# Decode attention with a streamed output projection: wo of two neighbouring groups in one transfer and one projection

## The chip, the cores and the metric

The kernel runs on one core of one Trainium2 chip. The metric is the device time of one execution in microseconds (us); lower is better. Each run also has a "span": the time from the first to the last instruction that the profile of that run shows, usually 1.2 us below the device time and free of what happens outside the program.

## The reference, cut to what matters

Two independent problems, A and B, are computed and concatenated. Each is one decode step of attention over the last 4096 keys of a cache, followed by an output projection.

```python
B, Sq, D = 2, 1, 576
Hq, Hkv, Sk, Dh = 32, 16, 16384, 128
W = 4096
q = (x @ wq)                                   # 2 rows, 32 heads of 128
k = repeat(k_cache[:, :, Sk - W:, :], 2)       # 16 kv heads, 4096 keys
v = repeat(v_cache[:, :, Sk - W:, :], 2)
p = softmax(q k^T * Dh ** -0.5)
o = p v
return o.reshape(B, Sq, Hq * Dh) @ wo          # wo: 4096 x 576
```

K and V are read once, 134 MB in all, and wq and wo are 19 MB more. There is little arithmetic for each byte.

## The kernel before

The work is cut into 8 groups (4 per problem) of 4 kv heads, that is 8 query heads, and a group into 2 slabs, one per batch row. A slab of K or V is one 4 MiB transfer (128 rows of 32 KB) into a ring of four slots. For each group there is also one "stripe" of wo, 1024 rows of 576 numbers: 128 partitions with 8 wo rows each, so 9 KB per partition. All these transfers go out on one queue in a fixed order:

```python
for t in range(NSLAB + LAG):                    # NSLAB = 16, LAG = 3
    if t < NSLAB:
        stream.append(("K", t))
    if t >= LAG:
        i = t - LAG
        if i % 2 == 0 and 0 < i // 2 < NG - 1:
            stream.append(("W", i // 2 - 1))    # a stripe of wo
        stream.append(("V", i))
stream.append(("W", NG - 2))                    # stripe 6
stream.append(("W", NG - 1))                    # stripe 7
# ... (cut)
if kind == "W":
    sl = i % 2                                  # two buffers of 8 rows
    rows = probs[P][4][gl * 1024:(gl + 1) * 1024, :].rearrange("(p j) n -> p j n", j=8)
    deps = [proj_op[i - 2]] if i >= 2 else []
    cuts = [(0, 8, wo_sem[sl])]
    if i == NG - 2:                             # stripe 6 in two pieces
        cuts = [(0, 4, wo_sem[sl]), (4, 8, lastw_sem[2])]
    elif i == NG - 1:                           # stripe 7 in three: 4, 3 and 1 rows
        cuts = [(w_cuts[k], w_cuts[k + 1], ([wo_sem[sl]] + lastw_sem)[k]) for k in range(3)]
```

`make_PV` multiplies the softmax weights with a slab of V. After the last V slab of a group, VectorE (DVE) reduces the result, PE multiplies it with a selection matrix (`make_dg`, "the select" below), and DVE masks and picks O into the layout that the projection needs (`make_pick`). The projection is 8 rows times 2 halves of the output, 16 matmuls of 288 columns.

The end of the program, in the order in which PE gets it:

```python
make_PV(i + 3, (0,))          # last V slab, first piece
make_dg(NG - 1, (0,)); make_pick(NG - 1, (0,))
filler(2)                     # two matmuls whose result nobody reads
make_PV(i + 3, (1, 2))        # last V slab, the other two pieces
make_evac(i + 3)
filler(2)
make_dg(NG - 1, (1,))         # the last select, waits for VectorE
make_pick(NG - 1, (1,))
make_proj(NG - 2)             # stripe 6
make_proj(NG - 1)             # stripe 7
make_E(NPROB - 1)             # copy out, output transfer
```

Of the kernel before, what the change touches and what calls it, by code (L numbers as in the profile page):

```python
# [62 lines left out]
def build_kernel(nc, probs, out):  # L63
# [29 lines left out]
    with es:  # L93
        sb = lambda name, shape, dt: es.enter_context(nc.sbuf_tensor(name, shape, dt))
        ring = sb("ring", [128, NSLOT, SW], BF16)
        xt = sb("xt", [128, 2, HW_], BF16)
        wob = sb("wob", [128, 2, 8, NOUT], BF16)
        zq = sb("zq", [128, 4, 4, 144], BF16)
        pR = sb("pR", [128, 2048], BF16)
        pT = sb("pT", [128, 2, 2048], BF16)  # L100
# [15 lines left out]
        jmask_f = sb("jmask_f", [128, 8], FP32)  # L116
        m8 = sb("m8", [128, 16, 8], FP32)
        selx = sb("selx", [128, 8, 16], FP32)
        bsel = sb("bsel", [128, 2], FP32)
        hmask = sb("hmask", [8, 2], FP32)  # L120
        mx = sb("mx", [128, 2], FP32)
# [7 lines left out]
        ssum = sb("ssum", [128, 2], FP32)  # L129
        rsb = sb("rsb", [128, 2, 2], FP32)  # L130
        oP = sb("oP", [128, 2, 8, Bb], BF16)
        part = sb("part", [Bb, NH], FP32)
        out_sb = sb("out_sb", [Bb, NPROB, NOUT], BF16)
        STT = [es.enter_context(nc.psum_tensor("st%d" % i, [128, 1024], FP32)) for i in range(2)]
# [20 lines left out]
        v_cuts = [0, 64, 112, KJ]  # L155
        lastv_sem = [sem("lastv%d" % k) for k in range(2)]
        w_cuts = [0, 4, 7, 8]
        lastw_sem = [sem("lastw%d" % k) for k in range(3)]
        wq_sem = [sem("wq%d" % P) for P in range(NPROB)]
        wo_sem = [sem("wo%d" % r) for r in range(2)]  # L160
        x_sem = sem("xload")
# [63 lines left out]
        p_v2 = pool(lambda e: e.tensor_tensor(v2[:], vmask[:, 0:2], vmask[:, 2:4], ALU.add), [d_vm], "v2")  # L225
        p_m8 = pool(lambda e: e.tensor_copy(m8[:], jmask_f[:, 0:8].unsqueeze(1).broadcast_to([128, 16, 8])), [d_jf], "m8")
        p_sx = pool(lambda e: e.tensor_copy(selx[:], jmask_f[:, 0:8].unsqueeze(2).broadcast_to([128, 8, 16])), [d_jf], "selx")

        tbn = [0]
        tb_consumer = {}  # L230
# [86 lines left out]
        for t in range(NSLAB + LAG):  # L317
            if t < NSLAB:
                stream.append(("K", t))
            if t >= LAG:  # L320
                i = t - LAG
                if i % 2 == 0 and 0 < i // 2 < NG - 1:
                    stream.append(("W", i // 2 - 1))
                stream.append(("V", i))
        stream.append(("W", NG - 2))
        stream.append(("W", NG - 1))
        slot_of = {}
        uses = {}
        n_slot = 0
        for key in stream:  # L330
            if key[0] != "W":
                slot_of[key] = (n_slot + 3) % NSLOT
                uses.setdefault(slot_of[key], []).append(key)
                n_slot += 1
# [1 line left out]
        stream_dma = {}  # L336
        last_reader = {}
        pos = [0]
        proj_op = {}

        def issue(key):
            kind, i = key
            if kind == "W":
                P, gl = i // GP, i % GP
                sl = i % 2
                rows = probs[P][4][gl * 1024:(gl + 1) * 1024, :].rearrange("(p j) n -> p j n", j=8)
                deps = [proj_op[i - 2]] if i >= 2 else []
                cuts = [(0, 8, wo_sem[sl])]
                if i == NG - 2:
                    cuts = [(0, 4, wo_sem[sl]), (4, 8, lastw_sem[2])]  # L350
                elif i == NG - 1:
                    cuts = [(w_cuts[k], w_cuts[k + 1], ([wo_sem[sl]] + lastw_sem)[k]) for k in range(3)]
                stream_dma[key] = []
                for j0, j1, sm in cuts:
                    def f(e, j0=j0, j1=j1, sm=sm):
                        return e.dma_start(wob[:, sl, j0:j1, :].rearrange("p j n -> p (j n)"),
                                           rows[:, j0:j1, :].rearrange("p j n -> p (j n)")).then_inc(sm, 16)
                    stream_dma[key].append((j0, j1, dma_op("sp", sm, 1, f, deps, "wo%d_%d" % (i, j0))))
                return
            P, g, b = i // (2 * GP), (i // 2) % GP, i % 2  # L360
            src_t = probs[P][1] if kind == "K" else probs[P][2]
            src = src_t[b, 4 * g:4 * g + 4, Sk - W:Sk, :].rearrange("k (r j) d -> r k j d", j=KJ)
            r = slot_of[key]
            prior = uses[r][:uses[r].index(key)]
            deps = [last_reader[prior[-1]]] if prior else first_deps[r]
            cuts = [(0, KJ, ring_sem[r])]
            if key == ("V", NSLAB - 1):
                cuts = [(v_cuts[k], v_cuts[k + 1], ([ring_sem[r]] + lastv_sem)[k]) for k in range(3)]
            stream_dma[key] = []
            for c0, c1, sm in cuts:  # L370
                def f(e, c0=c0, c1=c1, sm=sm):
                    return e.dma_start(ring[:, r, c0 * 128:c1 * 128],
                                       src[:, :, c0:c1, :].rearrange("r k j d -> r k (j d)")).then_inc(sm, 16)
                stream_dma[key].append((c0, c1, dma_op("sp", sm, 1, f, deps, "%s%d_%d" % (kind, i, c0))))
# [187 lines left out]

        def make_dg(G, bs=(0, 1)):
            b0, nb = bs[0], len(bs)
            n, bank, op = tb_job(lambda e, bank: e.matmul(bank[:, 0:128 * nb], selx[:].rearrange("p h c -> p (h c)"),  # L565
                                                          oR[:, b0:b0 + nb, :].rearrange("p b d -> p (b d)"), start=True, stop=True),
                                 "dg%d_%d" % (G, b0), [ch[(G, "red%d" % b)] for b in bs] + [p_sx])
            ch[(G, "dg")] = op
            dg_job[(G, bs)] = (n, bank)

        def make_pick(G, bs=(0, 1)):
            v = G % 2
            b0, nb = bs[0], len(bs)
            n, bank = dg_job[(G, bs)]
            tv = tmp[:, 0:128 * nb]
            a = dve(lambda e: e.tensor_tensor(
                tv.rearrange("p (b c j) -> p b c j", b=nb, c=16), bank[:, 0:128 * nb].rearrange("p (b c j) -> p b c j", b=nb, c=16),
                cm16[:, 0:16].unsqueeze(1).unsqueeze(3).broadcast_to([128, nb, 16, 8]), ALU.mult), [ch[(G, "dg")], d_cm, ch["tmp"]], "A%d" % G)
            tb_consumer[n] = a

            def f_pick(e):
                with nc.allow_low_precision(reason="one term of the sixteen is not zero"):
                    return e.tensor_reduce(oP[:, v, :, b0:b0 + nb].rearrange("p j b -> p b j"),
                                           tv.rearrange("p (b c j) -> p b j c", b=nb, c=16), AX.X, ALU.add)
            ch[(G, "oP", b0)] = dve(f_pick, [a] + ([proj_op[G - 2]] if G >= 2 else []), "oP%d_%d" % (G, b0))
            ch["tmp"] = ch[(G, "oP", b0)]

        def make_proj(G, part=None):
            P = G // GP
            v = G % 2  # L590
            start = G % GP == 0
            ensure(("W", G))
            oPs = [ch[(G, "oP", b)] for b in range(2) if (G, "oP", b) in ch]
            parts = stream_dma[("W", G)]
            for j0, j1, dma in parts if part is None else [parts[part]]:
                split = G == NG - 1 and j1 == 8
                for halves in ([(0,), (1,)] if split else [(0, 1)]):
                    def f(e, j0=j0, j1=j1, halves=halves):
                        for j in range(j0, j1):
                            wt = oP[:, v, j, :]  # L600
                            for h in halves:
                                mv_ = wob[:, v, j, h * NH:(h + 1) * NH]
                                if h == 1 and G >= NG - 2:
                                    last = e.matmul(PJL, wt, mv_, start=G == NG - 2 and j == 0, stop=True, skip_group_check=True)
                                elif h == 1:
                                    last = mm_held(e, PJ[h], wt, mv_, start and j == 0, ((128, 32), (0, 0)))
                                else:
                                    last = e.matmul(PJ[h], wt, mv_, start=start and j == 0, stop=True, skip_group_check=True)  # L608
                        return last
                    deps = oPs + [dma]  # L610
                    if start:
                        deps += [e_ops[(P - 1, 0)], e_ops[(P - 1, 1)]] if P >= 1 else [q_ev[2]]
                    op = pe(f, deps, "proj%d_%d" % (G, j0))
                    if split:
                        projh[halves[0]] = op
                    else:
                        proj_op[G] = op

        def make_part():
            ch["part"] = act(lambda e: e.activation(part[:], PJ[1], ACTF.Copy), [proj_op[NG - 3]], "part")  # L620

        def make_E(P):
            if P < NPROB - 1:
                d = [proj_op[(P + 1) * GP - 1]]
                e_ops[(P, 0)] = dve(lambda e: e.tensor_copy(out_sb[:, P, 0:NH], PJ[0]), d, "Elo%d" % P)
                e_ops[(P, 1)] = act(lambda e: e.activation(out_sb[:, P, NH:NOUT], PJ[1], ACTF.Copy), d, "Ehi%d" % P)
            else:
# [10 lines left out]
        for t in range(NSLAB):  # L638
# [26 lines left out]
                make_sums(Gs)  # L665
            if Gd is not None:
                make_dg(Gd)
            if Gp is not None:
                make_proj(Gp)
                if (Gp + 1) % GP == 0:  # L670
                    make_E(Gp // GP)
            if Gc is not None:
# [10 lines left out]
        make_bias(NG - 1)  # L683
        make_PV(i + 1)
        make_evac(i + 1)
        make_proj(NG - 3)
        make_part()
        make_dg(NG - 2)
        make_pick(NG - 2)
# [105 lines left out]
```

## Time and profile before

| | before |
|---|---|
| device time, median of 3 runs | 363.62 us (363.46 to 364.47) |
| span of the profiled run | 362.1 us |
| bytes read from HBM | 153.10 MB, 423 GB/s over the span |
| busy: PE, DVE, ACT | 65%, 59%, 13% |

The page of the profile, the rows of PE clock and DMA (one digit per fortieth of the span, in tenths) and the DMA packets:

```profile
PEclk9999699969898768969899889969698966898959
DMA  8999999999999999999999999999999999999996
DMA packets 6803, 153.26 MB, mean 423 GB/s; under 512 B 764, under 2 KB 904, under 8 KB 1544
```

The DMA row is at 9 from the second slice to the last but one. The core is a DMA stream with some arithmetic beside it. The PE clock moves between 6 and 9 tenths. These are means over a slice: the clock records of all traces hold only two values, 1.0 (full) and 0.5 (half), and all but the last of a trace, which the end cuts, are multiples of 3.41 us long.

The transfers of wo, with KB and the median time from issue to landing:

```profile
wob<-in_A_wo_dram SPq DMA_DIRECT2D x4, 1152.0 KB, 30.4
wob<-in_B_wo_dram SPq DMA_DIRECT2D x2, 1152.0 KB, 31.1
```

A transfer lands 30 us after its issue although it moves in 2.76 to 2.78 us (from the first engine's landing of the transfer ahead to its own): the queue was full.

The chain of work that ended last, its last pieces (start, duration, what):

```profile
340.44 19.13 DMA wob<-in_B_wo_dram
359.61 0.28 PE pj L608
...
360.26 0.05 PE pj L604
360.33 0.45 DVE out_sb L629
```

The chain names the last piece of wo but one, which landed at 359.57; the last one, a single row, landed at 359.92, in time for its matmuls at 359.97. So the run ends with the wo landings, a few matmuls, the copy. The timeline of PE there (start, duration, instruction, idle time before it in brackets):

```profile
356.35 0.49 PE L565 MATMUL tb<-oR,selx 128*128 128x128 f32 x2 [1.11 <-DVE oR L555]
356.77 0.28 PE L608 MATMUL pj<-wob,oP 128*2 128x288 bf16 x1
...
357.63 0.29 PE L604 MATMUL pj<-wob,oP 128*2 128x288 bf16 x1
358.67 0.28 PE L608 MATMUL pj<-wob,oP 128*2 128x288 bf16 x1 [0.76 <-DMA wob<-in_B_wo_dram]
...
359.61 0.28 PE L608 MATMUL pj<-wob,oP 128*2 128x288 bf16 x1 [0.28 <-DMA wob<-in_B_wo_dram]
...
359.98 0.29 PE L604 MATMUL pj<-wob,oP 128*2 128x288 bf16 x1
```

The last select ran at 356.35, then stripe 6 (16 matmuls, two at a time every 0.12 us). Then PE idled before stripe 7, whose two bracketed waits name the wo transfer. The tail followed the data.

Two waits that the prediction uses, one of the DMA queue's own and one of DVE:

```profile
SPq L356 <- PE pj L244: 10.7, 1, 10.7
```
```profile
313.55 0.23 DVE L484 SCALAR_TENSOR_TENSOR bias<-vmask,tb,offm 128x4 f32<-128x4 f32 x1 [7.60 <-PE tb L481]
```

For finer questions I use two kinds of record in the trace that have no view of their own: each DMA packet with its size, start and duration, and each of the 16 semaphore increments of a transfer (one per DMA engine), called landings below.

### The profile page before, as it was taken

The numbers are of one execution on the slowest core, as the hardware profiler recorded it, in microseconds if no ns is written. First come the engines' busy times: TensorE is split into PE (matmuls) and PEld (weight loads), VectorE is DVE, ScalarE is ACT, GpSimd is POOL, SyncE is SP. The second block draws the span as 40 slices with busy tenths as digits, with TensorE's granted clock in tenths as the row PEclk, the third lists the DMA queues.
The fourth block names the chain that finished last, engine by engine and source line by source line (L and its number), as shares of the span: only waits on it lengthen the run. The fifth ranks groups of instructions, "written<-read, shape, count | busy, mean of one in ns | idle before, by whom it ended". The sixth has DMA issues, their size and how long they took to land.

```text
span 362.1 us, 2631 instructions
## 1 busy us (share of the span) xinstructions
PE 234.5 (65%) x1294; PEld 57.2 (16%) x935; DVE 211.9 (59%) x141; ACT 46.1 (13%) x80; POOL 22.0 (6%) x82
## 2 busy tenths in 40 slices
PE   0397788567654957665684836665786627849575
PEld 0010111112110211211120201212121201202222
DVE  0201898495949093764939185772939367393732
ACT  1002100140041000500032000500005000320500
POOL 3100101100010000100010000100010001000000
PEclk9999699969898768969899889969698966898959
DMA  8999999999999999999999999999999999999996
GB/s 327 456 427 413 456 411 438 431 420 449 416 436 434 420 449 400 450 434 424 443 418 427 442 420 447 420 427 442 420 430 434 431 438 424 429 434 427 418 414 256
DMA packets 6803, 153.26 MB, mean 423 GB/s; under 512 B 764, under 2 KB 904, under 8 KB 1544
## 3 DMA queue, kind: packets, MB, share of 16 engines
q1 hardware_dynamic: 6772, 153.10, 98.7%
q8 instruction: 8, 0.13, 0.1%
q14 instruction: 3, 0.02, 0.0%
q10 hardware_dynamic: 20, 0.01, 0.0%
HBM read 153.10 MB, written 0.00 MB: 423 GB/s over the span
## 4 chain that ended last, share of the span: by engine, by line
DMA 54%; DVE 23%; PE 13%; issue 8%; ACT 1%; POOL 0%; ACTq 0%; SPq 0%
DMA ring<-in_B_k_cache_dram 32%; DMA ring<-in_A_k_cache_dram 14%; DVE xt L427 13%; DMA wob<-in_B_wo_dram 5%; PE st L244 4%; DMA tmp<-in_B_x_dram 3%; PE pj L244 3%; PE st L453 3%; DVE mx L461 2%; DVE oR L559 2%; ACT pR L491 1%; DVE tmp L552 1%; PE ot L275 1%; DVE pT L500 1%; PE ot L530 1%
## 5 line engine op out<-in xcount | busy, mean ns | idle before, releaser
L453 PE MATMUL st<-xt,zq 128*128 128x512 bf16 x256 | 120.9, 472 | 95.7 <-DVE xt L427 95.7
L427 DVE STREAM_TRANSPOSE xt<-ring 128x4096 f32<-128x4096 f32 x32 | 141.6, 4430 | 40.1 <-DMA ring<-in_A_k_cache_dram 23.4
L244 PE MATMUL st<-xt,zq 128*128 128x512 bf16 x256 | 119.6, 467 | 0.0
L491 ACT ACTIVATE pR<-st,bias 128x512 bf16<-128x512 f32 x32 | 40.0, 1419 | 227.5 <-DVE bias L484 227.5
L453 PEld LDWEIGHTS st<-xt,zq 128*128 128x128 bf16 x256 | 28.6, 112 | 216.6 <-DVE xt L427 112.6
L530 PE MATMUL ot<-ring,pT 128*32 128x512 bf16 x512 | 33.9, 408 | 2.9 <-DVE ssum L514 1.8
L484 DVE SCALAR_TENSOR_TENSOR bias<-vmask,tb,offm 128x4 f32<-128x4 f32 x8 | 1.8, 224 | 38.0 <-PE tb L481 38.0
L514 DVE TENSOR_REDUCE ssum<-tb 128x2 f32<-128x8 f32 x8 | 1.3, 162 | 36.8 <-PE tb L511 36.8
L500 DVE STREAM_TRANSPOSE pT<-pR 128x2048 bf16<-128x2048 bf16 x8 | 18.4, 2303 | 1.1 <-ACT pR L491 1.1
L419 POOL TENSOR_TENSOR zq<-qs,bmask 128x64 bf16<-128x64 bf16 x32 | 8.7, 294 | 163.2 <-PE st L244 140.9
L559 DVE TENSOR_REDUCE oR<-tmp 128x128 f32<-128x512 f32 x15 | 15.7, 1045 | 0.5
L530 PEld LDWEIGHTS ot<-ring,pT 128*32 128x32 bf16 x512 | 12.8, 100 | 19.3 <-DMA ring<-in_B_v_cache_dram 5.7
L552 DVE SCALAR_TENSOR_TENSOR tmp<-ot,rsb,dmask 128x512 f32<-128x512 f32 x16 | 11.5, 718 | 6.5 <-PE ot L530 6.5
L608 PE MATMUL pj<-wob,oP 128*2 128x288 bf16 x64 | 14.4, 285 | 1.0 <-DMA wob<-in_B_wo_dram 1.0
L244 PE MATMUL pj<-wob,oP 128*2 128x288 bf16 x48 | 12.0, 286 | 0.0
L244 PE MATMUL pj<-ring,pT 128*32 128x512 bf16 x36 | 11.8, 412 | 0.0
L254 PE MATMUL tb<-ident_b,pR 8*128 8x8 bf16 x9 | 0.7, 198 | 14.2 <-DVE pR L215 14.2
L461 DVE TENSOR_REDUCE mx<-st 128x2 f32<-128x1024 f32 x8 | 9.7, 1215 | 0.0
L491 ACT ACTIVATION_READ_ACCUMULATOR pR<-st,bias 128x1 f32 x32 | 9.0, 282 | 0.0
L565 PE MATMUL tb<-oR,selx 128*128 128x256 f32 (+1 forms) x18 | 6.2, 427 | 2.7 <-DVE ssum L514 1.5
L215 DVE TENSOR_TENSOR pR<-tmp,hmask 8x1152 bf16<-8x1152 bf16 x1 | 1.3, 1346 | 11.2 <-DMA tmp<-in_B_x_dram 11.2
L275 PE MATMUL ot<-ring,pT 128*32 128x512 bf16 x18 | 7.5, 419 | 0.5 <-ACT pT L261 0.5
(64 smaller groups left out, 71.0 us busy)
## 6 DMA issues: line engine op xcount, KB each, us to landing
ring<-in_A_k_cache_dram SPq DMA_DIRECT2D x8, 4096.0 KB, 28.0
ring<-in_A_v_cache_dram SPq DMA_DIRECT2D x8, 4096.0 KB, 30.1
ring<-in_B_k_cache_dram SPq DMA_DIRECT2D x8, 4096.0 KB, 28.9
ring<-in_B_v_cache_dram SPq DMA_DIRECT2D x7, 4096.0 KB, 30.6
ring<-in_A_wq_dram SPq DMA_DIRECT2D x1, 4608.0 KB, 13.6
ring<-in_B_wq_dram SPq DMA_DIRECT2D x1, 4608.0 KB, 24.0
wob<-in_A_wo_dram SPq DMA_DIRECT2D x4, 1152.0 KB, 30.4
wob<-in_B_wo_dram SPq DMA_DIRECT2D x2, 1152.0 KB, 31.1
```

Of the source, the lines that this page charges most:

```text
L244: return e.add_instruction(mybir.InstMatmult(name=nc.get_next_instruction_name(), engine=mybir.EngineType.PE, ins=[e.lower_ap(mv_), e.lowe ...
L275: last = e.matmul(QB[c], wt, mv_, start=first, stop=True, skip_group_check=True)
L419: last = e.tensor_tensor(dst, src, msk, ALU.mult)
L427: Xop[(t, jh)] = dve(lambda e: e.transpose(xt[:, jh, :].bitcast(FP32).rearrange("p (kp x kt) -> p x kp kt", kp=2, kt=2), ring[:, r, jh * H ...
L453: last = e.matmul(ob, wt, mv_, start=first, stop=True, skip_group_check=True)
L461: ch[(G, "max")] = dve(lambda e: e.tensor_reduce(mx[:], st[:, :].rearrange("p (x t) -> p t x", t=2), AX.X, ALU.max), [Sop[(2 * G + 1, 1)]] ...
L491: last = e.activation(pR[:].rearrange("p (x k) -> p k x", k=4)[:, kv, :], st[:, :].rearrange("p (x t) -> p t x", t=2)[:, kv % 2, :], ACTF.Exp,
L500: pT_op[G] = dve(lambda e: e.transpose(pT[:, v, :].rearrange("p (w j q) -> p j w q", w=4, q=8), pR[:].rearrange("p (j w q) -> p j w q", w= ...
L530: last = e.matmul(OTB[32 * c:32 * c + 32, :], pT[:, v, base + 32 * c:base + 32 * c + 32], ring[:, r, jj * 128:(jj + 4) * 128], start=rd == ...
L552: evac_op[i] = dve(lambda e: e.scalar_tensor_tensor(tv, o, rsb[:, v, b:b + 1], dm, ALU.mult, ALU.mult), deps, "ev%d" % i)
L559: ch[(G, "red%d" % b)] = dve(lambda e: e.tensor_reduce(oR[:, b, :], tmp[:].rearrange("p (j d) -> p d j", j=4), AX.X, ALU.add), [evac_op[i] ...
L608: last = e.matmul(PJ[h], wt, mv_, start=start and j == 0, stop=True, skip_group_check=True)
```

## The change

Its intent: fewer and longer packets. The stripes of two neighbouring groups are one transfer of 18 KB per partition, stripes 0 to 5 as three transfers. The two groups are projected together: 16 rows times 2 halves, 32 matmuls, once in two groups. To fit this layout the picked O of a group fills half the partitions (0 to 63 or 64 to 127), with 16 entries in place of 8. Stripes 6 and 7 stay single, but stripe 6 becomes one piece. Cut to its core:

```diff
-        wob = sb("wob", [128, 2, 8, NOUT], BF16)
+        wob = sb("wob", [128, 16, NOUT], BF16)
+        selm = sb("selm", [128, 16, 8], FP32)
+        oM = sb("oM", [128, 16, Bb], BF16)
 ... stream order
-                if i % 2 == 0 and 0 < i // 2 < NG - 1:
-                    stream.append(("W", i // 2 - 1))
+                if i % 4 == 0 and i > 0:
+                    stream.append(("M", i // 4 - 1))
 ... issue
+                n = 16 if kind == "M" else 8
+                rows = probs[P][4][gl * 1024:gl * 1024 + 128 * n, :].rearrange("(p j) n -> p j n", j=n)
+                deps = ([projm_op[i - 1]] if i >= 1 else []) if kind == "M" else [projm_op[NM - 1]]
-                if i == NG - 2:
-                    cuts = [(0, 4, wo_sem[sl]), (4, 8, lastw_sem[2])]
-                elif i == NG - 1:
+                if i == NG - 1:
 ... pick: half the partitions of a group
+            if G < NG - 2:
+                h0 = 64 * v
+                tv = tmp[h0:h0 + 64, 0:256]
 ... projection of two groups
+        def make_projm(q):
+                for j in range(16):
+                    for h in range(2):
+                        mv_ = wob[:, j, h * NH:(h + 1) * NH]
 ... in the loop, and after it
-            if Gp is not None:
-                make_proj(Gp)
+            if Gp is not None and Gp % 2 == 1:
+                make_projm(Gp // 2)
-        make_proj(NG - 3)
+        make_projm(NM - 1)
```

More of the change, by code (lines that the diff above doesn't have):

```diff
@@ L157, in build_kernel @@
         w_cuts = [0, 4, 7, 8]
-        lastw_sem = [sem("lastw%d" % k) for k in range(3)]
+        lastw_sem = [sem("lastw%d" % k) for k in range(2)]
         wq_sem = [sem("wq%d" % P) for P in range(NPROB)]
@@ L227, in build_kernel @@
         p_sx = pool(lambda e: e.tensor_copy(selx[:], jmask_f[:, 0:8].unsqueeze(2).broadcast_to([128, 8, 16])), [d_jf], "selx")
+        p_sm = pool(lambda e: e.tensor_copy(selm[:].rearrange("p (a h) c -> p a h c", a=2),
+                                            jmask_f[:, 0:8].unsqueeze(1).unsqueeze(3).broadcast_to([128, 2, 8, 8])), [d_jf], "selm")
         tbn = [0]
@@ L326, in build_kernel @@
         stream.append(("W", NG - 1))
+        NM = NG // 2 - 1
         slot_of = {}
@@ L330, in build_kernel @@
         for key in stream:
-            if key[0] != "W":
+            if key[0] in "KV":
                 slot_of[key] = (n_slot + 3) % NSLOT
@@ L338, in build_kernel @@
         pos = [0]
-        proj_op = {}
+        projm_op = {}
         def issue(key):
             kind, i = key
-            if kind == "W":
-                P, gl = i // GP, i % GP
-                sl = i % 2
-                rows = probs[P][4][gl * 1024:(gl + 1) * 1024, :].rearrange("(p j) n -> p j n", j=8)
-                deps = [proj_op[i - 2]] if i >= 2 else []
-                cuts = [(0, 8, wo_sem[sl])]
-                if i == NG - 2:
-                    cuts = [(0, 4, wo_sem[sl]), (4, 8, lastw_sem[2])]
-                elif i == NG - 1:
-                    cuts = [(w_cuts[k], w_cuts[k + 1], ([wo_sem[sl]] + lastw_sem)[k]) for k in range(3)]
+            if kind in "MW":
+                n = 16 if kind == "M" else 8
+                first_g = 2 * i if kind == "M" else i
+                P, gl = first_g // GP, first_g % GP
+                at = 0 if kind == "M" else 8 * (i % 2)
+                rows = probs[P][4][gl * 1024:gl * 1024 + 128 * n, :].rearrange("(p j) n -> p j n", j=n)
+                deps = ([projm_op[i - 1]] if i >= 1 else []) if kind == "M" else [projm_op[NM - 1]]
+                cuts = [(0, n, wo_sem[i % 2])]
+                if i == NG - 1:
+                    cuts = [(w_cuts[k], w_cuts[k + 1], ([wo_sem[1]] + lastw_sem)[k]) for k in range(3)]
                 stream_dma[key] = []
@@ L355, in f @@
                     def f(e, j0=j0, j1=j1, sm=sm):
-                        return e.dma_start(wob[:, sl, j0:j1, :].rearrange("p j n -> p (j n)"),
+                        return e.dma_start(wob[:, at + j0:at + j1, :].rearrange("p j n -> p (j n)"),
                                            rows[:, j0:j1, :].rearrange("p j n -> p (j n)")).then_inc(sm, 16)
@@ L564, in make_dg @@
             b0, nb = bs[0], len(bs)
-            n, bank, op = tb_job(lambda e, bank: e.matmul(bank[:, 0:128 * nb], selx[:].rearrange("p h c -> p (h c)"),
+            sl_, p_sl = (selx, p_sx) if G >= NG - 2 else (selm, p_sm)
+            n, bank, op = tb_job(lambda e, bank: e.matmul(bank[:, 0:128 * nb], sl_[:].rearrange("p h c -> p (h c)"),
                                                           oR[:, b0:b0 + nb, :].rearrange("p b d -> p (b d)"), start=True, stop=True),
-                                 "dg%d_%d" % (G, b0), [ch[(G, "red%d" % b)] for b in bs] + [p_sx])
+                                 "dg%d_%d" % (G, b0), [ch[(G, "red%d" % b)] for b in bs] + [p_sl])
             ch[(G, "dg")] = op
@@ L575, in make_pick @@
             tv = tmp[:, 0:128 * nb]
-            a = dve(lambda e: e.tensor_tensor(
-                tv.rearrange("p (b c j) -> p b c j", b=nb, c=16), bank[:, 0:128 * nb].rearrange("p (b c j) -> p b c j", b=nb, c=16),
-                cm16[:, 0:16].unsqueeze(1).unsqueeze(3).broadcast_to([128, nb, 16, 8]), ALU.mult), [ch[(G, "dg")], d_cm, ch["tmp"]], "A%d" % G)
+            if G < NG - 2:
+                h0 = 64 * v
+                tv = tmp[h0:h0 + 64, 0:256]
+                a = dve(lambda e: e.tensor_tensor(
+                    tv.rearrange("p (b c j) -> p b c j", b=2, c=8), bank[h0:h0 + 64, 0:256].rearrange("p (b c j) -> p b c j", b=2, c=8),
+                    jmask_f[h0:h0 + 64, 0:8].unsqueeze(1).unsqueeze(3).broadcast_to([64, 2, 8, 16]), ALU.mult),
+                    [ch[(G, "dg")], d_jf, ch["tmp"]], "A%d" % G)
+                dst, q = oM[h0:h0 + 64, :, :].rearrange("p j b -> p b j"), G // 2
+                free, c = [projm_op[q - 1]] if q >= 1 else [], 8
+            else:
+                a = dve(lambda e: e.tensor_tensor(
+                    tv.rearrange("p (b c j) -> p b c j", b=nb, c=16), bank[:, 0:128 * nb].rearrange("p (b c j) -> p b c j", b=nb, c=16),
+                    cm16[:, 0:16].unsqueeze(1).unsqueeze(3).broadcast_to([128, nb, 16, 8]), ALU.mult), [ch[(G, "dg")], d_cm, ch["tmp"]], "A%d" % G)
+                dst = oP[:, v, :, b0:b0 + nb].rearrange("p j b -> p b j")
+                free, c = [], 16
@@ L579, in make_pick @@
             tb_consumer[n] = a
             def f_pick(e):
-                with nc.allow_low_precision(reason="one term of the sixteen is not zero"):
-                    return e.tensor_reduce(oP[:, v, :, b0:b0 + nb].rearrange("p j b -> p b j"),
-                                           tv.rearrange("p (b c j) -> p b j c", b=nb, c=16), AX.X, ALU.add)
-            ch[(G, "oP", b0)] = dve(f_pick, [a] + ([proj_op[G - 2]] if G >= 2 else []), "oP%d_%d" % (G, b0))
+                with nc.allow_low_precision(reason="one term of the c is not zero"):
+                    return e.tensor_reduce(dst, tv.rearrange("p (b c j) -> p b j c", b=nb, c=c), AX.X, ALU.add)
@@ L586, in make_pick, with f @@
+            ch[(G, "oP", b0)] = dve(f_pick, [a] + free, "oP%d_%d" % (G, b0))
             ch["tmp"] = ch[(G, "oP", b0)]
-        def make_proj(G, part=None):
-            P = G // GP
+        def make_projm(q):
+            P, start = 2 * q // GP, (2 * q) % GP == 0
+            ensure(("M", q))
+            def f(e):
+                for j in range(16):
+                    for h in range(2):
+                        mv_ = wob[:, j, h * NH:(h + 1) * NH]
+                        if h == 1:
+                            last = mm_held(e, PJ[h], oM[:, j, :], mv_, start and j == 0, ((128, 32), (0, 0)))
+                        else:
+                            last = e.matmul(PJ[h], oM[:, j, :], mv_, start=start and j == 0, stop=True, skip_group_check=True)
+                return last
+            deps = [ch[(2 * q, "oP", 0)], ch[(2 * q + 1, "oP", 0)], stream_dma[("M", q)][0][2]]
+            if start:
+                deps += [e_ops[(P - 1, 0)], e_ops[(P - 1, 1)]] if P >= 1 else [q_ev[2]]
+            projm_op[q] = pe(f, deps, "projm%d" % q)
@@ L590, in make_proj @@
+        def make_proj(G):
             v = G % 2
-            start = G % GP == 0
             ensure(("W", G))
             oPs = [ch[(G, "oP", b)] for b in range(2) if (G, "oP", b) in ch]
-            parts = stream_dma[("W", G)]
-            for j0, j1, dma in parts if part is None else [parts[part]]:
+            for j0, j1, dma in stream_dma[("W", G)]:
                 split = G == NG - 1 and j1 == 8
@@ L601, in f @@
                             for h in halves:
-                                mv_ = wob[:, v, j, h * NH:(h + 1) * NH]
-                                if h == 1 and G >= NG - 2:
-                                    last = e.matmul(PJL, wt, mv_, start=G == NG - 2 and j == 0, stop=True, skip_group_check=True)
-                                elif h == 1:
-                                    last = mm_held(e, PJ[h], wt, mv_, start and j == 0, ((128, 32), (0, 0)))
-                                else:
-                                    last = e.matmul(PJ[h], wt, mv_, start=start and j == 0, stop=True, skip_group_check=True)
-                        return last
-                    deps = oPs + [dma]
-                    if start:
-                        deps += [e_ops[(P - 1, 0)], e_ops[(P - 1, 1)]] if P >= 1 else [q_ev[2]]
-                    op = pe(f, deps, "proj%d_%d" % (G, j0))
+                                mv_ = wob[:, 8 * v + j, h * NH:(h + 1) * NH]
+                                last = e.matmul(PJL if h else PJ[0], wt, mv_, start=h == 1 and G == NG - 2 and j == 0, stop=True, skip_group_check=True)
+                        return last
+                    op = pe(f, oPs + [dma], "proj%d_%d" % (G, j0))
                     if split:
                         projh[halves[0]] = op
-                    else:
-                        proj_op[G] = op
         def make_part():
-            ch["part"] = act(lambda e: e.activation(part[:], PJ[1], ACTF.Copy), [proj_op[NG - 3]], "part")
+            ch["part"] = act(lambda e: e.activation(part[:], PJ[1], ACTF.Copy), [projm_op[NM - 1]], "part")
         def make_E(P):
             if P < NPROB - 1:
-                d = [proj_op[(P + 1) * GP - 1]]
+                d = [projm_op[(P + 1) * GP // 2 - 1]]
                 e_ops[(P, 0)] = dve(lambda e: e.tensor_copy(out_sb[:, P, 0:NH], PJ[0]), d, "Elo%d" % P)
```

## The prediction

> **What bounds the kernel.** One DMA stream. In the page's 40 slices the DMA row is 9 except at both ends; the table of stretches gives DMA share 1.00 at 429 to 436 GB/s from 20 to 340 us, while PE is 65% and DVE 59% busy (page, first part). In the landing records a 4 MiB slab lands every 9.71 us (432 GB/s)[...]. The queue never runs dry: slabs land 28 to 31 us after issue (page, last part). So only bytes, per-packet cost, ramp and tail count.
>
> **The stream.** The bytes stay. In the packet records an engine takes a median of 1216 ns for 32,768 B, 349 for 9,216 B, 182 for 4,608 B, 9 for a semaphore packet. A line through the first two is 9.9 ns plus 36.8 ns per 1000 B: 688 ns for 18,432 B against 2 x 349 = 698. An engine carries 8 rows of each transfer. Estimates:
> - three merged pairs: 3 x (8 x 9.9 + 9) = 0.26 us;
> - stripe 6 in one piece: 8 x (2 x 182 - 349) + 9 = 0.13 us.
> About 0.35 to 0.4 us in all, 0.1% of the run, all on the critical path, since the stream ends last.
>
> **Off the path.**
> - Projection: the same matmuls (2 us per group, one every 0.12 us, timeline), now in bursts of 32.
> - Picks: the same 256 elements per partition (0.42 and 0.62 us) on half the partitions; same times expected. One more POOL copy at setup (0.3 us).
> - The merged buffer is single, but in program order a K slab that can only go after the projection stands ahead of the next transfer: no wait expected. At the end the issue wait on the projection (10.7 us in the queue's waits) now covers stripe 6 too; 14 us of V are still queued then.
>
> **The tail.** The last burst grows by 2 us, but group 4's projection no longer precedes the bias transpose at 313.3 us (VectorE waited 7.60 us for it), so the last chain starts about 1.2 us earlier (slab landed 312.5, its transpose began 313.7). Net +0.2 to 0.5 us before the last two PV, where PE waits for data anyway. Stripe 6's matmuls ran from 356.8 to 357.9, held by the last select (data landed by 357.1), and PE then waited 0.76 us for stripe 7; in one piece nothing backs up. The end stays: last wo landing, four rows, copy, output.
>
> **Predicted: 363.3 us**, range 362.7 to 364.0; the three runs before span 1.0 us, more than the effect. Chances: faster 0.01, within 2% 0.98, slower 0.01.
>
> **What would show it.**
> - packets 6,803 to about 6,227, under 8 KB 1,544 to about 1,224; 384 packets of 18,432 B at about 689 ns;
> - slab spacing 9.71 us still, a merged transfer about 5.5 us where two took 2.8 each; DMA row unchanged;
> - the 7.60 us wait about 2 us shorter;
> - PE still idle before stripe 7; the chain still ends in DMA wo, PE projection, copy.
>
> **What would make it wrong.** A delay of the last chain over 1 us (select, stripe 6 and 7 then queue up after the data landed): up to 1 us slower. A stall of the issuing queue on the single buffer. A changed slowest engine: the last engine's landing trails the first's by 1.9 us, grown in jumps of up to 0.9 us, some near the 16 KB instruction fetches that share the engines; a shifted fetch could move the end some tenths either way.

## The result

| | before | changed |
|---|---|---|
| device time, median of 6 runs | 363.73 us (363.46 to 364.68) | 363.85 us (363.46 to 364.63) |
| ratio, 95% interval | | 0.9999 (0.9983 to 1.0015) |
| span of the profiled run | 362.1 us | 362.7 us |

A ratio here is the mean time of one kernel's runs over that of the other's of the same rounds, so it is not quite the ratio of the medians. The time is the same; nothing can be told apart at 0.15%. The results are correct.

The page of the changed kernel, the same rows:

```profile
PEclk9999698969898888986798989889789687889986
DMA  8999999999999999999999999999999999999995
DMA packets 6228, 153.28 MB, mean 423 GB/s; under 512 B 700, under 2 KB 840, under 8 KB 1224
```

```profile
wob<-in_A_wo_dram SPq DMA_DIRECT2D x2, 2304.0 KB, 29.8
wob<-in_B_wo_dram SPq DMA_DIRECT2D x1, 2304.0 KB, 27.4
```

There are 575 packets fewer and the DMA row is as full as before. The chain that ended last, its last pieces (gaps of up to 0.04 us left out):

```profile
326.55 27.52 DMA ring<-in_B_v_cache_dram
354.12 0.43 PE ot L535 x4
354.57 0.76 DVE tmp L557
355.35 0.44 DVE tmp L559
355.81 0.30 DVE oR L560
356.16 0.79 PE tb L571 x2
356.96 4.00 PE pj L635 x32
360.98 0.45 DVE out_sb L651
```

This is not the chain of before. No wo transfer stands in it. It runs from the last V piece through DVE and the select into 32 matmuls that take 4.00 us without a gap. The same in the timeline of PE:

```profile
356.16 0.79 PE L571 MATMUL tb<-oR,selx 128*128 128x128 f32 x2 [0.71 <-DVE oR L560]
356.91 4.00 PE L635 MATMUL pj<-wob,oP 128*2 128x288 bf16 x32
```

Four microseconds for 16 pairs are 0.25 us per pair, where before had 0.12. The table of stretches gives the reason in its column PEclk (1.00 is full clock). Before:

```profile
core 0: us, PE busy (x) PEld busy (x) DVE busy (x) ACT busy (x) POOL busy (x), PEclk, DMA share, GB/s
100.00:340.00 240.00, 157.77 (x914) 40.09 (x682) 149.49 (x98) 33.20 (x54) 12.67 (x45) 0.86 1.00 430
351.00:354.40 3.40, 2.97 (x23) 0.93 (x19) 0.67 (x2) 0.00 (x0) 0.00 (x0) 0.56 1.01 409
354.60:357.90 3.30, 2.19 (x24) 1.00 (x19) 2.15 (x5) 0.00 (x0) 0.00 (x0) 1.00 1.00 402
358.20:361.30 3.10, 1.31 (x16) 0.55 (x16) 0.45 (x1) 0.40 (x1) 0.00 (x0) 1.00 0.21 81
```

Changed (same columns):

```profile
100.00:340.00 240.00, 158.69 (x915) 40.37 (x683) 149.46 (x98) 35.42 (x57) 12.77 (x46) 0.85 1.00 431
351.00:354.40 3.40, 1.16 (x17) 0.33 (x16) 0.36 (x1) 0.00 (x0) 0.00 (x0) 1.00 1.00 410
354.60:357.90 3.30, 2.59 (x14) 1.07 (x14) 2.12 (x5) 0.00 (x0) 0.00 (x0) 0.50 0.98 397
358.20:361.30 3.10, 2.71 (x24) 1.20 (x18) 0.33 (x1) 0.36 (x1) 0.00 (x0) 0.50 0.19 67
```

Between 100 and 340 us the two kernels are alike: clock 0.86 and 0.85, DMA share 1.00. After 354.6 us before had full clock and changed half clock (from 351.0 to 354.4 it was the other way round). The two waits, of the queue and of DVE, that were shown of before:

```profile
SPq L361 <- PE pj L248: 13.2, 1, 13.2
```
```profile
312.46 0.23 DVE L489 SCALAR_TENSOR_TENSOR bias<-vmask,tb,offm 128x4 f32<-128x4 f32 x1 [5.46 <-PE tb L486]
```

The queue's wait on the projection grew from 10.7 to 13.2 us, but 14 us of V were still queued: stripe 6 was issued at 340.4 us, and the last V piece landed at 354.07. The wait of DVE for the last bias shrank from 7.60 to 5.46 us.

Where the 0.65 us between the two profiled spans come from, by the landing records (last engine of each transfer): the first slab landed 0.21 us later (35.20 for 34.99), the stream from there to the last piece of wo was 0.43 us shorter (324.50 for 324.93), and from that landing to the end it took 0.87 us longer (3.02 for 2.15). The sum is 0.65.

### The profile page after: what moved, and what is told of

It reads as the page before. It is cut to its first block, busy times and chain, and to the rows that moved or that the text cites. A ratio compares the mean times of both kernels' runs of the same rounds, so it can differ in the third digit from the quotient of the medians.

```text
span 362.7 us, 2629 instructions
## 1 busy us (share of the span) xinstructions
PE 237.2 (65%) x1295; PEld 58.2 (16%) x935; DVE 211.9 (58%) x141; ACT 46.2 (13%) x80; POOL 22.1 (6%) x83
## 2 busy tenths in 40 slices
DMA packets 6228, 153.28 MB, mean 423 GB/s; under 512 B 700, under 2 KB 840, under 8 KB 1224
## 4 chain that ended last, share of the span: by engine, by line
DMA 48%; DVE 25%; PE 16%; issue 8%; ACT 1%; SPq 0%; POOL 0%; ACTq 0%
DMA ring<-in_B_k_cache_dram 25%; DVE xt L432 15%; DMA ring<-in_A_k_cache_dram 13%; DMA ring<-in_B_v_cache_dram 8%; PE st L248 5%; PE st L458 4%; DMA tmp<-in_B_x_dram 3%; PE pj L248 3%; DVE oR L564 2%; DVE mx L466 2%; DVE pT L505 2%; DVE tmp L557 2%; ACT pR L496 1%; PE ot L279 1%; PE pj L635 1%
## 5 line engine op out<-in xcount | busy, mean ns | idle before, releaser
L458 PE MATMUL st<-xt,zq 128*128 128x512 bf16 x256 | 122.6, 479 | 89.9 <-DVE xt L432 89.8
L248 PE MATMUL st<-xt,zq 128*128 128x512 bf16 x256 | 121.2, 473 | 0.0
L535 PE MATMUL ot<-ring,pT 128*32 128x512 bf16 x512 | 32.5, 395 | 6.9 <-DMA ring<-in_B_v_cache_dram 4.4
L248 PE MATMUL pj<-wob,oM 128*2 128x288 bf16 x48 | 11.9, 286 | 0.0
L616 PE MATMUL pj<-wob,oM 128*2 128x288 bf16 x48 | 11.9, 286 | 0.0
L279 PE MATMUL ot<-ring,pT 128*32 128x512 bf16 x18 | 7.5, 419 | 0.5 <-ACT pT L265 0.5
L248 PE MATMUL st<-ring,pT 128*32 128x512 bf16 x18 | 7.3, 407 | 0.0
```

Of the source, the lines that this page charges most:

```text
L248: return e.add_instruction(mybir.InstMatmult(name=nc.get_next_instruction_name(), engine=mybir.EngineType.PE, ins=[e.lower_ap(mv_), e.lowe ...
L279: last = e.matmul(QB[c], wt, mv_, start=first, stop=True, skip_group_check=True)
L458: last = e.matmul(ob, wt, mv_, start=first, stop=True, skip_group_check=True)
L535: last = e.matmul(OTB[32 * c:32 * c + 32, :], pT[:, v, base + 32 * c:base + 32 * c + 32], ring[:, r, jj * 128:(jj + 4) * 128], start=rd == ...
L616: last = e.matmul(PJ[h], oM[:, j, :], mv_, start=start and j == 0, stop=True, skip_group_check=True)
```

## The experiments

The rivals, in short. **Theory A**: the stream became shorter by a few tenths, but the end does not always follow it. In some runs PE has half clock in the last microseconds, of either kernel, and then PE sets the end. **Rival B**: stripe 6 in one piece lands too late and lengthens the tail. **Rival C**: the longer rows save nothing.

The table is the sum of all runs; the sections below refer to it. "Above 362.65" counts runs whose span is above 362.65 us: the slow runs, or those with a slow tail, if nothing else is said. The experiments ran in three sets, on three chips by the record (e1 to e4, e5 to e8, e9 to e12), each with 11 runs of before; the mean span of before was 362.48, 362.66 and 362.46 us in them, so a difference of 0.2 us between sets proves little. Only one run of each kernel and set has a trace. No slow run of before itself was profiled; the slow tails seen in traces are those of the changed kernel (362.7), e10 (363.0) and e3 (the kernel before with short rows).

```
kernel                                    runs  span us, mean  median  lowest  highest  above 362.65
before                                      33      362.54     362.3    362.1    363.2      13
before, stripe 6 in one piece (e2, e11)     11      362.56     362.6    362.1    363.2       5
before, new order (e8, e12)                 12      362.31     362.3    362.1    362.6       0
changed (with e5)                           12      362.35     362.25   361.9    363.3       2
changed, stripe 6 in two pieces (e1, e10)   11      362.28     362.1    361.8    363.0       3
changed, two pieces, new order (e4, e9)     11      362.04     362.0    361.9    362.3       0
changed, more filler (e6)                    5      362.38     362.4    361.9    362.8       2
changed, no filler (e7)                      6      362.35     362.4    361.8    362.9       1
before, short rows (e3)                      6      364.02     364.05   363.4    364.5       6
```

And the stream by the landing records of the traces, in us; I chose this measure after the runs (see e1). The first column is the interval in which the first engine to land moves the six stripes 0 to 5, summed; the second the same for stripe 6.

```
                                  stripes 0 to 5   stripe 6
six transfers (5 traces, mean)        16.63      2.86 in two pieces, 2.80 in one
three transfers (8 traces, mean)      16.48      2.86 in two pieces, 2.79 in one
1152 B packets (e3)                   17.66      2.86
```

### e1 and e10: undo the one piece

```diff
-        lastw_sem = [sem("lastw%d" % k) for k in range(2)]
+        lastw_sem = [sem("lastw%d" % k) for k in range(3)]
                 cuts = [(0, n, wo_sem[i % 2])]
+                if kind == "W" and i == NG - 2:
+                    cuts = [(0, 4, wo_sem[0]), (4, 8, lastw_sem[2])]
```

> The changed kernel with stripe 6 again in two pieces (0 to 4, 4 to 8); the select matmul still ahead of it on PE. Theory A (the stream got about 0.4 us shorter, but the last projections wait for PE, at half clock in the profiled run, so the end does not follow the stream): the stream is about 0.13 us longer than with one piece, the last select still holds stripe 6 until about 356.4 us, and the time is within 0.2 us of the changed kernel's 363.85. If PE has half clock in the tail, 16 projection pairs back to back at 0.24 us, if full clock 0.12 us and idle before stripe 7. Rival B (stripe 6 in one piece lands too late and delays the tail by 0.5 us or more): about 0.5 us faster, 363.3 or less. Rival C (merging saves nothing): last-engine stream from the first V slab to the last wo piece as long as before, 324.9 us.

Measured: 363.64 us, ratio to before 0.9996 (0.9983 to 1.0009), and all five spans between 361.8 and 362.1. The profiled run had full clock and 2.16 us from the last landing to the end. The tight spans looked like rival B's, so the same kernel ran again later:

> e1 once more (merged, stripe 6 in two pieces, old order), for more runs. Rival B (splitting stripe 6 alone keeps the tail short): all spans 361.8 to 362.2 again. Theory A (the split without the new order does nothing, e1's five short runs were luck): two groups as in the changed kernel, about a third of the runs at 362.4 and up.

Measured: 364.19 us, ratio 1.0006 (0.9992 to 1.0020), three of six spans at 362.9 to 363.0. The five short runs of e1 were luck, then: with e10 the count is 3 slow runs of 11. The profiled run was one of the slow ones:

```profile
351.00:354.40 3.40, 1.15 (x17) 0.34 (x16) 0.46 (x2) 0.00 (x0) 0.00 (x0) 0.96 0.99 401
354.60:357.90 3.30, 2.62 (x14) 0.95 (x11) 1.98 (x5) 0.00 (x0) 0.00 (x0) 0.50 0.97 391
358.20:361.30 3.10, 2.96 (x26) 1.40 (x22) 0.08 (x1) 0.11 (x1) 0.00 (x0) 0.56 0.19 72
```

```profile
355.72 0.44 DVE tmp L561
356.18 0.30 DVE oR L562
356.52 0.79 PE tb L573 x2
357.31 3.89 PE pj L637 x32
```

Half clock from 354.1 on, 32 matmuls in 3.89 us, 3.06 us from the last landing to the end, with stripe 6 in two pieces. So the slow tail does not need the one piece, and rival B does not explain it. Rival C is a harder case. By the yardstick of its own expectation it is not refuted: the stream to the last engine's landing, 324.93 us before, was 324.88 in e1, and over all traces it is 324.50 to 324.97 with three transfers and 324.85 to 325.06 with six. What speaks against it is the first engine's landing, by which the six stripes take 0.15 us less in three transfers in every trace (16.45 to 16.50 for 16.61 to 16.66), and the spans of e9 against e12 below.

### e2 and e11: only stripe 6 in one piece

```diff
                 cuts = [(0, 8, wo_sem[sl])]
-                if i == NG - 2:
-                    cuts = [(0, 4, wo_sem[sl]), (4, 8, lastw_sem[2])]
-                elif i == NG - 1:
+                if i == NG - 1:
```

> The kernel before with stripe 6 in one piece and nothing else. Theory A: last-engine stream from the first V slab to the last wo piece 0.13 us shorter than 324.93, about 324.8; time within 0.2 us of the kernel before; the tail depends only on PE's clock after 354 us. Rival B: slower than before by 0.5 us or more, also with full clock in the tail.

> e2 once more (kernel before, stripe 6 in one piece), for more runs. Rival B (one piece lengthens the tail): again most spans 362.6 and up (4 of 5 in e2). Theory A: mixed as in the kernel before, about half below 362.4.

Measured: 364.03 us, ratio 1.0005 (0.9993 to 1.0017), four of five spans at 362.7 to 363.0; then 363.87 us, ratio 1.0006 (0.9990 to 1.0022), with two of six above 362.4. Both profiled runs had full clock in the tail and ended 2.15 and 2.13 us after the last landing, as before does: with full clock the one piece costs nothing. Stripe 6 moved in 2.80 us for 2.86, but the stream to the last engine's landing was 324.96 and 324.90 us, not the 324.8 expected. The slow runs were not profiled. The number of slow runs (7 of 11 above 362.35, where before has 14 of 33) is too small a difference to say whether the one piece makes the slow mode more frequent; that stays open.

### e3: eight packets where there was one

```diff
-  rows = ....rearrange("(p j) n -> p j n", j=8)
+  rows = ....rearrange("(p j) n -> p j n" if i >= NG - 2 else "(j p) n -> p j n", j=8)
+                        if i < NG - 2:
+                            return e.dma_start(wob[:, sl, j0:j1, :], rows[:, j0:j1, :]).then_inc(sm, 16)
```

> The kernel before with the rows of wo stripes 0 to 5 in pieces of 1152 B (eight packets a row where there was one; the rows land at other partitions, so the result is wrong on purpose). Packets of 1152 B took 51 ns in the profile before, one of 9216 B 349 ns: 6 stripes x 8 rows x (8 x 51 - 349) = 2.8 us. Theory A (cost per packet lies on the critical path, one for one): 2.8 us slower, about 366.5, the landing of such a stripe 3.27 us after the slab ahead instead of 2.79. Rival C (the stream hides packet cost): under 0.5 us slower.

Measured: the result is wrong; 365.33 us, ratio 1.0044 (1.0029 to 1.0060), lowest span 363.4 where before has 362.1. It is slower by 1.3 us in the lowest span and by 1.5 in the mean of its set, part of that the slow tail described below, and not by 2.8. Cost per packet does lie on the critical path, but in the stream it is less than half of what I took it for. The landings say how much: the six stripes took 17.66 us for 16.63 with 336 packets more on each engine (6 x 8 x 7), which is 3.1 ns per packet. (The edit also changes the order in which wo is read from HBM; what that costs was not separated.) The packet records still say 51 ns for 1152 B, and 64 of those would be 3.27 us, but a stripe moved in about 2.95: the durations overlap, so their fixed part (9.9 ns by the line in the prediction) is not what a packet costs the stream. The spans also fall into two groups (363.4 to 363.7 and 364.4 to 364.5), and the profiled run of the second group had half clock from 356.0 on and 3.02 us from landing to end.

### e4 and e9: stripe 6 in two pieces, the first before the last select

This takes e1 and moves one thing: the projection of the first piece comes where PE waits for DVE.

```diff
         filler(2)
+        make_proj(NG - 2, (0,))
         make_dg(NG - 1, (1,))
         make_pick(NG - 1, (1,))
-        make_proj(NG - 2)
+        make_proj(NG - 2, (1,))
         make_proj(NG - 1)
```

> The changed kernel with stripe 6 in two pieces and the projection of its first piece ahead of the last select on PE, in the time in which PE waits for VectorE. Theory A: at half clock PE has only 12 pairs (2.9 us) left after the select in place of 16 (3.8 us), so the end comes within 0.9 us of the last wo landing, in every run; spans 361.7 to 362.2 us; median time 0.3 to 0.5 us below the changed kernel, and no gain in a run whose tail has full clock. Rival B: the same gain as from splitting alone (e1). If the tail is not PE-bound (neither): no difference from e1.

> e4 once more (merged, stripe 6 in two pieces, its first piece projected before the last select), for more runs. Theory A with the order of the tail as the cure: all spans 361.8 to 362.2 again. If the five tight spans of e4 were luck: one or more spans of 362.4 and up.

Measured: 363.30 us, ratio 0.9990 (0.9976 to 1.0004); then 363.70 us, ratio 0.9997 (0.9985 to 1.0010). All 11 spans lie between 361.9 and 362.3 (one at 362.3, a tenth above what I had expected). The gain of 0.3 to 0.5 us in median device time is not shown: 363.30 and 363.70 us stand against 363.85 and 363.40 of the changed kernel. The profile of e4:

```profile
351.00:354.40 3.40, 1.15 (x17) 0.33 (x16) 0.46 (x2) 0.00 (x0) 0.00 (x0) 1.00 1.00 405
354.60:357.90 3.30, 3.23 (x22) 1.16 (x19) 1.76 (x5) 0.00 (x0) 0.00 (x0) 0.51 0.97 389
358.20:361.30 3.10, 1.50 (x20) 0.55 (x16) 0.53 (x2) 0.40 (x1) 0.00 (x0) 1.00 0.16 62
```

```profile
341.85 17.68 DMA wob<-in_B_wo_dram
359.58 0.70 PE pj L638 x8
360.31 0.45 DVE out_sb L654
```

Compare this with e10 and with the changed kernel. All three had half clock in the stretch from 354.6 on. There PE was busy for 3.23 us of 3.30 in e4, 2.62 in e10 and 2.59 in the changed kernel; in the next stretch e4 had full clock and the other two half clock (e10 got full clock only at 360.9). So the new order does two things: eight of the matmuls are done before the select, and PE is busy enough that the clock comes back one step earlier. The chain ends in a wo transfer again, PE is done 0.4 us after the last landing (expected: within 0.9), and the end comes 2.15 us after it. That the matmuls done early brought the clock back is read from this one trace and e12's; no run separates it from the shorter rest.

### e8 and e12: the new order in the kernel before

```diff
         filler(2)
+        make_proj(NG - 2, 0)
         make_dg(NG - 1, (1,))
         make_pick(NG - 1, (1,))
-        make_proj(NG - 2)
+        make_proj(NG - 2, 1)
         make_proj(NG - 1)
```

> The kernel before with one thing moved: the projection of stripe 6's first piece ahead of the last select on PE, as in e4; wo as before (six transfers of 9 KB rows). If the order of the tail is what counts: no half-clock mode, spans within 0.3 us of each other, about 362.1 to 362.3, and 0.1 to 0.2 us above e4 (361.9 to 362.1), which is what the merged transfers give. If the merge is worth the 0.26 us of the prediction: 0.26 us or more above e4. If the order does not count: two groups as in the kernel before, 362.2 and 363.0.

> e8 once more (kernel before, first piece of stripe 6 projected before the last select), for more runs. If the order shortens the slow mode: no span above 362.7 (the kernel before has 363.0 to 363.2 in 8 of 22 runs), and the shortest 0.15 to 0.25 us above the shortest of e9, which is what the merge gives.

Measured: 363.81 us, ratio 0.9999 (0.9983 to 1.0016), and 363.67 us, ratio 1.0001 (0.9987 to 1.0014). No span of 12 is above 362.6, but e8's spread is 0.5 us where 0.3 was expected. The trace of e12 is the counterpart of e4's in the kernel before: half clock from 354.8 to 358.2, PE busy for 3.21 us of 3.30 there, full clock after it, and an end 2.14 us after the last landing. Over all kernels, the old order has 23 of 67 spans above 362.65 (the short rows left out, whose stream is longer; fillers left out), the new order none of 23. This is the experiment that shows where the slow tail lies: on PE, in the work around the last select. The new order is not full protection: the profiled run of e8 lost the full clock only at 358.9, and its tail was 2.61 us. That it shows a difference in spans is clear; in device time, with its scatter of more than 1 us, the ratios show none.

Medians and lowest spans of the two kernels with the new order differ by 0.3 and 0.2 us (362.3 to 362.0, 362.1 to 361.9). In the means it is 0.27 us (standard error 0.06), and 0.20 for e12 and e9, which ran in the same set. Apart from e8's tail the tails are the same, so this is what the merged transfers are worth in the span. It is clear of zero, but it can't decide between the 0.15 us of the landings and the 0.26 of the prediction.

### e5: the changed kernel again

> The changed kernel once more, for more runs and a second trace. Theory A (two modes by PE's clock in the last microseconds): core spans fall into two groups, about 362.0 (full clock, about 2.15 us from the last wo landing to the end) and about 362.6 (half clock, about 3.0 us); the first batch had 2 and 4 of 6. The trace shows one of the two tails, and the granted clock after 355 us says which. Rival (a slower tail by something else, e.g. the DMA itself): spans of one group, or a long tail with full clock.

Measured: 363.40 us, ratio 0.9987 (0.9971 to 1.0003). Five spans at 361.9 to 362.3, one at 363.3. The trace shows a third kind of tail, 2.41 us, which I had not expected: half clock from 345.6 to 355.9, so PE reached the last V piece late, the last select ran at 357.9 where it ran at 356.2 in the first trace, and the 32 matmuls followed in 2.12 us at full clock. So two groups is too simple. The half clock can cost time before the select (this trace, 2.41 us), in the last projections (the first trace, 3.02 us), or not at all (before, at half clock from 343.8 to 354.0 us, 2.15 us), according to where its steps fall.

### e6 and e7: more idle-time matmuls, and none

```diff
-        filler(2)      # e6: 6 and 4; e7: both lines taken out
+        filler(6)
         make_PV(i + 3, (1, 2))
         make_evac(i + 3)
-        filler(2)
+        filler(4)
```

> The changed kernel with six idle-time matmuls in place of two after the first piece of the last PV, and four in place of two after the last. If half clock in the tail follows a PE that idled in the 3.4 us before ([...] the clock records come in steps of 3.41 us): full clock in the tail in nearly all runs, spans 361.7 to 362.2, median 0.4 to 0.6 us below the changed kernel. If half clock follows a PE that worked too much: more half-clock tails, spans 362.5 and up.

> The changed kernel without the idle-time matmuls. If half clock follows an idle PE: half clock in the tail in nearly all runs, spans about 362.6, median 363.9 or more, tail of about 3.0 us in the trace. If it follows too much work: full clock, spans about 362.0.

Measured: e6 363.90 us, ratio 0.9991 (0.9977 to 1.0005), spans 361.9 to 362.8; e7 363.63 us, ratio 0.9989 (0.9976 to 1.0003), spans 361.8 to 362.9. Both expectations missed: with many fillers slow runs remain, without them fast runs remain, and the tail of e7's trace was 2.64 us, not 3.0. (That half clock follows an idle PE was my conjecture in these expectations, not shown before the runs.) The two traces do not contradict the idea that an idle PE loses the clock (in e7 PE was busy for 52% of the step before 358.3, and the clock was halved there), but how often it happens is not governed by these fillers. Why e6 still has slow runs is open: none of them was profiled.

To see without new runs what goes with a change of the clock, I cut all 14 traces from 40 us on into steps of 3.413 us, aligned with the changes in the clock records, and took the share of each step in which PE was busy and the clock of the next one:

```
clock in the step -> in the next     steps   PE busy share: lowest, median, highest
full -> full                           661        0.41  0.72  1.00
full -> half                           268        0.00  0.29  0.55
half -> full                           273        0.77  1.00  1.00
half -> half                            99        0.00  0.38  0.80
```

In these traces full clock was lost only after steps with PE busy for 0.55 or less (median 0.29), and came back only after steps of 0.77 or more (median 1.00); between 0.41 and 0.55 it was sometimes kept and sometimes lost, and between 0.77 and 0.80 half clock was sometimes kept and sometimes left. In the changed kernel the step before 354.5 had 0.36 and the one before 357.9 had 0.79, and half clock followed both; in e4 the one before 358.1 had 0.98, and full clock followed. These shares come from modelled ends of matmuls and are a correlation, but they separate with little overlap. The two experiments that set out to steer the clock, e6 and e7, did not succeed, so that the half clock is what makes a tail slow is read from traces and not shown by a run that switches it.

## Why the prediction was right or wrong, point by point

- **Time, "363.3 us", within 2%**: measured 363.85 and 363.40 us in two sets of six, inside the range of 362.7 to 364.0. That says little: the range of 1.3 us is over three times the predicted effect, and any forecast of "no visible change" would have fallen in it. The 0.3 us by which 363.3 lies under before can't be seen in device time (363.85 against 363.73 in the same rounds). "Same" was right, and the reason for it, that per-packet cost is a small matter in a stream at 432 GB/s, was right.
- **What bounds the kernel**: right. The DMA row, the slab spacing of 9.71 us and the stretch from 100 to 340 us are unchanged.
- **"three merged pairs: 0.26 us" and "stripe 6 in one piece: 0.13 us"**: the direction was right. Measured by the first engine's landings both terms were too large: 0.15 us and 0.07 us. (For the first, the spans of e8 and e12 against e4 and e9, 0.20 to 0.27 us, do not exclude 0.26.) The failing step is the 9.9 ns per packet from the line through packet durations. Durations of neighbouring packets overlap (in e3 64 of them sum to 3.27 us where the stripe took about 2.95); e3 measured 3.1 ns per extra packet in the stream. At that rate the 24 packets that the merge removes are 0.07 us; what the other half of the 0.15 us is (each merge also removes 16 packets under 512 B, one per engine, of 9 ns each) was not separated.
- **Packet counts**: predicted 6,227 in all and 1,224 under 8 KB; the page has 6,228 and 1,224. The 18,432 B packets took a median of 688 ns (predicted 689), a merged transfer 5.5 us (predicted 5.5).
- **Off the path**: the bursts of 32, the picks on half the partitions (0.42 and 0.58 us for 0.42 and 0.62) and the single buffer cost nothing. The wait on the last bias shrank by 2.1 us (predicted about 2). The last chain did start 1.1 us earlier (transpose at 312.6 for 313.7).
- **The tail, "in one piece nothing backs up", "PE still idle before stripe 7", "the chain still ends in DMA wo"**: wrong in the profiled run, right in others. I had read matmul pairs of 0.12 us from a trace in which the tail had full clock, and taken that for the kernel's tail. At half clock, 16 pairs behind the last select need 3.9 us, the data only 2.8, and PE sets the end: 3.02 us after the last landing in place of 2.15. The prediction had named this shape of failure ("select, stripe 6 and 7 then queue up"), but from a chain delayed by over 1 us; here the select was not late (356.16 us for 356.35), but its matmuls and the projections behind it ran at half clock. This cost of up to 0.9 us comes and goes from run to run, in the changed kernel by its traces, in before by its spans only, and it is larger than the gain. With the scatter outside the span, which reaches 1.5 us, it is why the gain of about 0.2 us in the stream (last landing 359.82 us after the start, mean of the four traces of the changed kernel and its filler variants, to 360.00, mean of three with wo as before) can't be seen in the time. Over all runs the mean span fell by 0.19 us (362.54 to 362.35), which fits, but is not clear of the scatter by itself.

- **"Jumps of up to 0.9 us"** between the first and the last engine's landing: in the landing records of that trace the largest is 0.80 us. Its slab landed from 53.88 to 55.32 us, and a 16 KB instruction fetch began at 48.55, in the interval before. As each of the eight such fetches of the trace ended, a data packet began that took longer than the others: 1.68 to 1.76 us for 32 KB (median 1.22), 0.81 to 0.88 us for 9 KB (median 0.35). The end did not turn on it.

The version with the tightest and lowest spans is e4: mean 362.04, 0.5 us (0.14%) under before. Within each of its two sets the difference is 0.50 and 0.38 us. In device time its two ratios, 0.9990 and 0.9997, do not clear the noise.

## What to carry to other kernels

In a stream with full queues, cost a change in packets by the spacing of landings, not by packet durations, which overlap: the durations overstated the cost of an extra short packet about three times here (9.9 ns by the line, 3.1 ns by e3). Before you call a difference of half a microsecond an effect, look at the granted PE clock in the last stretch of each trace, and at the spans of all runs: here about a third of the runs in the old order (23 of 67) ended late, and in every trace of a late end that I have it was PE that ended it. Work that can be done while PE waits should stand before the wait in program order: in e4 this left 12 pairs of matmuls behind the last select in place of 16, and PE was busy for 3.23 us of the 3.30 from 354.6 on, where it was 2.59 in the changed kernel.
